# Streamed weights by single blocks in a ring of sixteen half-size slots

## The chip, the cores and the metric

The kernel runs on one core of a Trainium2 chip. The metric is the device time in microseconds from the first to the last instruction of that core. Five engines work beside each other: TensorE (PE, matmuls, with its weight loads listed as PEld), VectorE (DVE), ScalarE (ACT), GpSimd (POOL) and SyncE (SP), which here only issues transfers. Sixteen DMA engines carry the transfers between the chip's memory (HBM) and the on-chip buffer.

## The reference, cut to what matters

Two layers, each used twice in turn, A, B, A, B, with a residual around each. A is attention over segments of 32 tokens: each segment sees 8 memory tokens that come out of the segment before it, so the 64 segments of a layer are worked one after the other, and each needs all of the layer's weights (Wq, Wk, Wv and Wo, 31.5 MB together). B is a mixer with two small matmuls and a shift of tokens, followed by an MLP.

```python
# A: S = 2048 tokens, Dm = 640, H = 32 heads of Dh = 192, M = 8, seg_len = 32
for s in range(n_seg):
    xs = x[:, s * seg_len:(s + 1) * seg_len, :].copy()
    h = jnp.concatenate([mem, xs], axis=1)
    q = jnp.einsum('btd,dhe->bhte', h, Wq)
    k = jnp.einsum('btd,dhe->bhte', h, Wk)
    v = jnp.einsum('btd,dhe->bhte', h, Wv)
    scores = jnp.einsum('bhqe,bhke->bhqk', q, k) * scale
    scores = jnp.where(mask[None, None], scores, -1000000000.0)
    p = _softmax(scores, axis=-1)
    o = jnp.einsum('bhqk,bhke->bhqe', p, v)
    o = jnp.einsum('bhte,hed->btd', o, Wo)
    mem = o[:, :M, :].copy()
    outs.append(o[:, M:, :])
# B (D = 640, F = 1536)
h = _gelu(_layernorm(x, axis=-1) @ w1)
# ... hs = (h, each quarter of its columns shifted along the tokens) @ w2 ...
x1 = x + hs
h2 = _gelu(_layernorm(x1, axis=-1) @ w3) @ w4
# the whole: x + A(ln(x)), then x + B(ln(x)), then both once more
```

## The kernel before

Both uses of A run in one pass as two lanes: step t works segment t of the first use and segment t - 5 of the second, side by side in one matmul of 80 columns (2 x (32 + 8)), so a weight block that is loaded serves both. There are 64 + 5 = 69 steps. A step goes through eight groups of four heads. A weight block is 128 rows by 768 columns (k, q, v: five blocks a group) or 128 x 640 (o: six blocks a group, and all blocks of the mixer). The on-chip buffer doesn't hold all weights: of each group the first blocks stay (`CUT`), and the others are streamed from HBM at each step through a ring of slots.

```python
LAG = 5
HG = 4
RING = 8
RING_A = 7
RING_B = 3
CUT = {"k": [3] * 8, "q": [3] * 8, "v": [3] * 8, "o": [2] + [4] * 7}
# ...
DMA_RATE = 345.0e3
DMA_LAT = 2.2
DMA_SKEW = 1.6
FLIGHT = 5
```

`RING` is the number of slots of the ring; attention may hold 7 of them at once and the mixer 3. A slot has room for two blocks.

```python
    def ring(cls):
        b = Slotted(cls, None)
        b.make = lambda: wring.tile([P, 2 * GW], bf16, name="wst", tag=f"r{b.slot}")
        return b

    def block(t, kind, g, c, due):
        n = Dm if kind == "o" else GW
        cut = CUT[kind][g]
        if c < cut:
            # ... resident: one load of the first `cut` blocks, once ...
            return b, lambda: tl[:, c, :]
        a = cut + (c - cut) // 2 * 2
        if (t, kind, g, a) not in streamed:
            b = ring("ra")

            def fn(op):
                return nc.sync.dma_start(out=T(b)[:, 0:2 * n].rearrange("p (c n) -> p c n", c=2), in_=w_src(kind, g, a, a + 2))
            add("SP", 0.45, due, fn, w=(b,), dma=P * 2 * n * 2, queue="wa")
            streamed[t, kind, g, a] = b
        b = streamed[t, kind, g, a]
        return b, lambda: T(b)[:, (c - a) * n:(c - a + 1) * n]
```

`load_b` does the same for the mixer's blocks (w1, w2, w3, w4), also by twos. A block is used by a run of matmuls, of which each loads 128 x 128 of it:

```python
            for kc in range(KC):
                due = due0 + kc * 0.05
                wb, wv = block(t, "v", g, kc, due)

                def fv(op, wv=wv, kc=kc):
                    w, o = wv(), T(pv)
                    for c in range(GC):
                        nc.tensor.matmul(out=o[:, c, 0:N], lhsT=w[:, c * P:(c + 1) * P], rhs=h[:, kc, c0:c0 + N],
                                         start=pv.begin(), stop=True, skip_group_check=True)
```

The kernel doesn't write its instructions in program order. It records all operations with an estimated duration and a due time, lays them out on the engines once in Python (`Plan.place`), and then emits them in that fixed order. The plan, and at the end the program too, lets a weight transfer start only when the one `FLIGHT` places before it has landed:

```python
            if o.dma and o.e == "SP" and len(landed) >= FLIGHT:
                s = max(s, landed[-FLIGHT])
# ...
    for o in placed:
        ins = o.fn(o)
        if o.dma and o.e == "SP":
            if len(flight) >= FLIGHT:
                tc.add_manual_dep(ins.ins, flight[-FLIGHT].ins.name,
                                  mybir.DependencyInfo(mybir.DependencyClass.Sync, mybir.DependencyReason.DATA),
                                  reason="transfers in flight")
            flight.append(ins)
```

The semaphore waits that carry the order between engines and slots are set when the program is built.

Of the kernel before, what the change touches and what calls it, by code (L numbers as in the profile page):

```python
# [12 lines left out]
bf16 = mybir.dt.bfloat16  # L13
# [6 lines left out]

LAG = 5
HG = 4
RING = 8
RING_A = 7
RING_B = 3
CUT = {"k": [3] * 8, "q": [3] * 8, "v": [3] * 8, "o": [2] + [4] * 7}
YA = 3
STEP = 48.0
# [11 lines left out]
LOOK = 0.03  # L40
DMA_RATE = 345.0e3
DMA_LAT = 2.2
DMA_SKEW = 1.6
FLIGHT = 5


class Buf:
# [34 lines left out]
class Plan:  # L82
# [11 lines left out]
    def add(self, e, d, due, fn, r=(), w=(), a=(), dma=0, queue=None, after=()):  # L94
        op = Op()
        op.e, op.d, op.due, op.fn, op.dma = e, d, due, fn, dma
        op.succ, op.ready, op.n = [], 0.0, 0
        op.i = len(self.ops)
        preds = set(after)
        slots = []  # L100
        for b in r:
            preds.update(b.writers)
        for b in w:
            preds.update(b.writers)
            preds.update(b.readers)
        for b in a:
            preds.update(b.base)
            preds.update(b.readers)
        for b in r:
            b.readers.append(op)  # L110
        for b in w:
            b.base = [op]
            b.writers = [op]
            b.readers = []
        for b in a:
            b.writers.append(op)
        for b in {id(b): b for b in (*r, *w, *a)}.values():
            if isinstance(b, Slotted):
                b.left += 1
                slots.append(b)  # L120
        op.slots = slots
        preds.discard(op)
        for p in preds:
            p.succ.append(op)
            op.n += 1
        self.ops.append(op)
        if queue is not None:
            self.queues.setdefault(queue, []).append(op)
        return op

    def place(self):
# [28 lines left out]
        def est(o, t):  # L160
            s = max(t, o.ready)
            if o.dma and o.e == "SP" and len(landed) >= FLIGHT:
                s = max(s, landed[-FLIGHT])
            need = {}
# [11 lines left out]
        while left:  # L176
# [33 lines left out]
            if o.dma:  # L210
                srv = max(s + DMA_LAT, srv) + o.dma / DMA_RATE
                done = srv + DMA_SKEW
                if e == "SP":
# [33 lines left out]
def kernel(  # L247
# [16 lines left out]
    nc = tc.nc  # L264
    P = 128
    _, S, Dm = A_x.shape
# [5 lines left out]
    KC = Dm // P  # L272
    FC = F // P
    assert (Dm, F, Dh, H, SEG, M) == (640, 1536, 192, 32, 32, 8) and S % (2 * SEG) == 0 and NSEG > 8
    NG = H // HG
    GW = HG * Dh
# [6 lines left out]
    QD = Dm // 4  # L283
# [12 lines left out]
    w4_v = B_w4.rearrange("(c p) n -> p c n", p=P)  # L296
# [3 lines left out]
    wring = ctx.enter_context(tc.tile_pool(name="wring", bufs=1))  # L300
# [4 lines left out]
    wbd = dram.tile([KC + FC + 1, P, Dm], bf16, name="wbd")  # L305
# [74 lines left out]
    def B(*key):  # L380
        if key not in bufs:
            bufs[key] = Buf()
        return bufs[key]

    plan = Plan({**PSUM_BANKS, "r": RING}, {**PSUM_USES, "ra": ("r", RING_A), "rb": ("r", RING_B)})
    add = plan.add
# [9 lines left out]
    def T(b):  # L396
        if b.obj is None:
            b.obj = b.make()
        return b.obj
# [12 lines left out]
    def w_src(kind, g, a, e):  # L412
        if kind == "o":
            return Wo_v[:, g, a:e, :]
        return W_v[kind][:, a:e, GW * g:GW * (g + 1)]

    resident = {}
    streamed = {}

    def ring(cls):  # L420
        b = Slotted(cls, None)
        b.make = lambda: wring.tile([P, 2 * GW], bf16, name="wst", tag=f"r{b.slot}")
        return b

    def block(t, kind, g, c, due):
# [4 lines that stand above are left out]
            if (kind, g) not in resident:  # L430
                tl = wres.tile([P, cut, n], bf16, name=f"w{kind}{g}")
                b = Buf()

                def fn(op):
                    return nc.sync.dma_start(out=tl[:], in_=w_src(kind, g, 0, cut))
                add("SP", 0.45, due, fn, w=(b,), dma=P * cut * n * 2, queue="wa")
                resident[kind, g] = b, tl
            b, tl = resident[kind, g]
            return b, lambda: tl[:, c, :]
        a = cut + (c - cut) // 2 * 2  # L440
        if (t, kind, g, a) not in streamed:
            b = ring("ra")

            def fn(op):
                return nc.sync.dma_start(out=T(b)[:, 0:2 * n].rearrange("p (c n) -> p c n", c=2), in_=w_src(kind, g, a, a + 2))
            add("SP", 0.45, due, fn, w=(b,), dma=P * 2 * n * 2, queue="wa")
            streamed[t, kind, g, a] = b
        b = streamed[t, kind, g, a]
        return b, lambda: T(b)[:, (c - a) * n:(c - a + 1) * n]

    mixer = {}

    def load_b(c, nm, n, due):

        a = n - n % 2
        e = min(a + 2, KC if nm in ("w1", "w2") else FC)
        if (c, nm, a) not in mixer:
            b = ring("rb")
            k = {"w1": a, "w3": KC + a, "w2": KC + FC - 4 + a}.get(nm)
            if nm == "w4":  # L460
                src, rd = w4_v[:, a:e, :], []
            elif nm == "w2" and a < 4:
                src, rd = B_w2.rearrange("(g r) d -> r g d", r=QD)[0:P, a:e, :], []
            else:
                src = wbd[k:k + e - a].rearrange("b p n -> p b n")
                rd = [B("wbd", k + i) for i in range(e - a)]

            def fn(op):
                return nc.sync.dma_start(out=T(b)[:, 0:(e - a) * Dm].rearrange("p (c n) -> p c n", n=Dm), in_=src)
            add("SP", 0.45, due, fn, r=rd, w=(b,), dma=P * (e - a) * Dm * 2, queue="wb")  # L470
            mixer[c, nm, a] = b
        b = mixer[c, nm, a]
        return b, lambda: T(b)[:, (n - a) * Dm:(n - a + 1) * Dm]

    def order_mixer_weights():

# [35 lines left out]
    def attention_step(t):  # L512
# [11 lines left out]
        def proj_kq(g, s0):  # L524
            G = t * NG + g
            for kind, off in (("k", 0.0), ("q", 0.3 * sl)):
                pq = ps("P", [P, GC, NS], f32, "ps" + kind)
                now = []
                for kc in range(KC):
                    due = s0 + off + kc * 0.05  # L530
                    wb, wv = block(t, kind, g, kc, due)

                    def fn(op, pq=pq, wv=wv, kc=kc):
                        w, o = wv(), T(pq)
                        for c in range(GC):
                            nc.tensor.matmul(out=o[:, c, 0:N], lhsT=w[:, c * P:(c + 1) * P], rhs=h[:, kc, c0:c0 + N],  # L536
                                             start=pq.begin(), stop=True, skip_group_check=True)
                    now.append(add("PE", mm_us(N, k=GC), due, fn, r=(wb, *HX(t, kc)), a=(pq,), after=last[0]))
# [25 lines left out]
        def proj_v(g, due0):  # L564
# [5 lines left out]
# [9 lines that stand above are left out]
                now.append(add("PE", mm_us(N, k=GC), due, fv, r=(wb, *HX(t, kc)), a=(pv,), after=last[0]))  # L579
# [17 lines left out]
        def attend(g):  # L597
# [66 lines left out]
            held = g >= NG - OT_BUFS + 1  # L664
            at = base + STEP - HOLD + 0.5 * g if held else s0 + 1.9 * sl
            ws = [block(t, "o", g, c, at + 0.03 * c) for c in range(GC)]
            due = base + STEP - 1 + 0.02 * g if held else s0 + 2.0 * sl

# [178 lines left out]
    def chunk(c):  # L847
# [110 lines left out]
        for n in range(5):  # L958
            due = D(W2[0] + W2[1] * n)
            wb, wv = load_b(c, "w2", n, due)  # L960

            def fw(op, n=n, wv=wv):
                w = wv()
                off = W2OFF[n] if n < 4 else 0
                lhsT = hTB[:, n, off:off + TOK, :].rearrange("p w l -> p (w l)")
                for k in range(2):
                    nc.tensor.matmul(out=T(hs[k])[:], lhsT=lhsT, rhs=w[:, HC * k:HC * (k + 1)],  # L967
                                     start=hs[k].begin(), stop=True, skip_group_check=True)
            add("PE", mm_us(HC, k=2), due, fw, r=(wb, B("hTB", 0), B("hTB", 1)), a=tuple(hs))
# [130 lines left out]
# [6 lines that stand above are left out]
# [37 lines left out]
```

## Time and profile before

| | |
|---|---|
| time, median of three runs | 3589.97 us (3584.36 to 3591.39) |
| span of the profiled run | 3584.0 us |
| TensorE's granted clock, mean | 0.99 |
| moved by DMA | 1097 MB, 306 GB/s on average |
| shares of the chain that ended last | PE 86%, DMA 8%, issue 4% |
| streamed transfers | 2,277 pairs of attention blocks, 630 transfers of mixer blocks, 32 resident loads and 2 others |
| landing of a streamed attention pair, median | 5.0 to 5.2 us after its issue |

The page gives for each engine its busy time and share of the span; lists of waits give, for each group of instructions, what ended its idle time, with the sum in us, how often, and the longest. "issue" in place of a releaser means that nothing was found for which the engine waited. The DMA table counts packets: the rows of a transfer are packets of 1,536 or 1,280 bytes, and q1 is the queue that SyncE fills, q0 that of GpSimd, q8 and q14 carry instructions. In a timeline a row is a start, a duration, and the instructions merged in it. The transfer time to landing runs from the issue on SyncE to the last completion.

### The profile page before, as it was taken

The numbers are of one execution on the slowest core, as the hardware profiler recorded it, in microseconds if no ns is written. First come the engines' busy times: TensorE is split into PE (matmuls) and PEld (weight loads), VectorE is DVE, ScalarE is ACT, GpSimd is POOL, SyncE is SP. The second block draws the span as 40 slices with busy tenths as digits, with TensorE's granted clock in tenths as the row PEclk, the third lists the DMA queues.
The fourth block names the chain that finished last, engine by engine and source line by source line (L and its number), as shares of the span: only waits on it lengthen the run. The fifth ranks groups of instructions, "written<-read, shape, count | busy, mean of one in ns | idle before, by whom it ended". The sixth has DMA issues, their size and how long they took to land.

```text
span 3584.0 us, 188496 instructions
## 1 busy us (share of the span) xinstructions
PE 3387.8 (95%) x84703; PEld 3256.1 (91%) x84703; DVE 2375.3 (66%) x7085; ACT 1709.2 (48%) x3584; POOL 306.2 (9%) x522
## 2 busy tenths in 40 slices
PE   5889999999999999999999999999999999999996
PEld 4778999999999999999999999999999999999875
DVE  2456767767667666776666777776667667776555
ACT  2344545545455544455445554554545445544432
POOL 2000000000000000000000000000000000000000
PEclk9999999999999999999999999999999999999998
DMA  9999999999999999999999999999999999999996
GB/s 341 314 308 306 309 298 309 306 302 315 307 310 323 310 299 304 303 301 312 303 305 310 303 299 303 313 312 300 310 318 309 302 304 306 308 309 310 321 310 212
DMA packets 804793, 1097.18 MB, mean 306 GB/s; under 512 B 51982, under 2 KB 800540, under 8 KB 803984
## 3 DMA queue, kind: packets, MB, share of 16 engines
q1 hardware_dynamic: 795472, 1069.06, 91.2%
q0 software_dynamic: 8512, 16.08, 1.4%
q8 instruction: 662, 10.85, 1.2%
q14 instruction: 147, 1.20, 0.1%
HBM read 1079.68 MB, written 8.19 MB: 304 GB/s over the span
## 4 chain that ended last, share of the span: by engine, by line
PE 86%; DMA 8%; issue 4%; DVE 0%; ACT 0%; POOL 0%; SPq 0%; POOLq 0%; DVEq 0%; ACTq 0%
PE psy L675 16%; PE psk L536 15%; PE psv L577 15%; PE psq L536 15%; PE psvt L589 5%; PE pso L656 4%; PE pss L608 4%; PE psh L999 3%; DMA wst<-in_B_w_dram 3%; PE y L1017 3%; PE pst L641 2%; DMA wst<-in_A_Wk_dram 2%; PE hs L967 1%; DMA wst<-in_A_Wv_dram 1%; PE psh L945 1%
## 5 line engine op out<-in xcount | busy, mean ns | idle before, releaser
L536 PEld LDWEIGHTS <-wst 128*128 128x128 bf16 x13248 | 561.5, 100 | 36.0 <-issue 19.3
L662 DVE CAST oT<-pso 128x480 bf16<-128x480 f32 (+1 forms) x552 | 341.7, 619 | 379.7 <-PE pso L656 377.3
L593 ACT COPY V<-psvt 80x768 bf16<-80x768 bf16 (+1 forms) x552 | 438.4, 794 | 309.0 <-PE psvt L589 302.2
L675 PE MATMUL psy<-oT,wo 128*128 128x80 bf16 (+1 forms) x10350 | 491.6, 199 | 15.3 <-issue 8.6
L577 PE MATMUL psv<-hT,wv 128*128 128x80 bf16 (+1 forms) x9936 | 480.5, 199 | 12.3 <-issue 10.7
L544 ACT CAST qT<-psq 128x480 bf16<-128x480 f32 (+1 forms) x552 | 292.1, 529 | 400.5 <-PE psq L536 398.9
L536 PE MATMUL psq<-hT,wq 128*128 128x80 bf16 (+1 forms) x9936 | 454.2, 199 | 19.6 <-issue 10.0
L583 ACT CAST vTs<-psv 128x480 bf16<-128x480 f32 (+1 forms) x552 | 291.2, 528 | 362.7 <-PE psv L577 359.5
L536 PE MATMUL psk<-hT,wk 128*128 128x80 bf16 (+1 forms) x9936 | 452.8, 199 | 11.7 <-issue 9.3
L619 DVE CUSTOM_DVE_ANT_1 pss<-pss,mask 80x320 f32<-80x320 f32 (+1 forms) x512 | 246.0, 481 | 294.3 <-PE pss L608 287.8
L577 PEld LDWEIGHTS <-wv 128*128 128x128 bf16 x9936 | 408.4, 99 | 30.0 <-issue 11.0
L675 PEld LDWEIGHTS <-wo 128*128 128x128 bf16 x10350 | 413.3, 99 | 23.4 <-issue 15.3
L536 PEld LDWEIGHTS <-wq 128*128 128x128 bf16 x9936 | 395.2, 100 | 31.2 <-issue 13.3
L536 PEld LDWEIGHTS <-wk 128*128 128x128 bf16 x9936 | 397.9, 100 | 25.4 <-issue 14.3
L536 PE MATMUL psk<-hT,wst 128*128 128x80 bf16 (+1 forms) x6624 | 367.9, 199 | 12.1 <-issue 6.5
L577 PE MATMUL psv<-hT,wst 128*128 128x80 bf16 (+1 forms) x6624 | 353.2, 199 | 12.4 <-issue 8.2
L675 PE MATMUL psy<-oT,wst 128*128 128x80 bf16 (+1 forms) x6210 | 335.4, 199 | 11.2 <-issue 10.4
L536 PE MATMUL psq<-hT,wst 128*128 128x80 bf16 (+1 forms) x6624 | 331.6, 199 | 12.4 <-issue 9.4
L626 ACT ACTIVATE pss<-pss,sm 80x320 f32<-80x320 f32 (+1 forms) x552 | 262.0, 475 | 151.5 <-DVE sm L619 151.5
L631 DVE TENSOR_REDUCE sm<-pss 80x4 f32<-80x320 f32 (+1 forms) x552 | 252.3, 457 | 116.4 <-ACT pss L626 115.7
L552 DVE CAST kT<-psk 128x320 bf16<-128x320 f32 (+1 forms) x552 | 254.0, 460 | 112.7 <-PE psk L536 109.3
L646 ACT COPY PT<-pst 80x320 bf16<-80x320 bf16 (+1 forms) x552 | 221.9, 402 | 220.2 <-PE pst L641 218.1
(117 smaller groups left out, 5256.9 us busy)
## 6 DMA issues: line engine op xcount, KB each, us to landing
wst<-in_A_Wk_dram SPq DMA_DIRECT2D x552, 384.0 KB, 5.2
wst<-in_A_Wq_dram SPq DMA_DIRECT2D x552, 384.0 KB, 5.2
wst<-in_A_Wv_dram SPq DMA_DIRECT2D x552, 384.0 KB, 5.2
wst<-in_A_Wo_dram SPq DMA_DIRECT2D x621, 320.0 KB, 5.0
wst<-wbd SPq DMA_DIRECT2D x280, 320.0 KB, 5.1
wst<-in_B_w_dram SPq DMA_DIRECT2D x280, 320.0 KB, 5.7
wst<-wbd SPq DMA_DIRECT2D x70, 160.0 KB, 4.4
wk<-in_A_Wk_dram SPq DMA_DIRECT2D x8, 576.0 KB, 6.8
```

Source lines behind the costliest of these rows:

```text
L536: nc.tensor.matmul(out=o[:, c, 0:N], lhsT=w[:, c * P:(c + 1) * P], rhs=h[:, kc, c0:c0 + N], start=pq.begin(), stop=True, skip_group_check= ...
L544: nc.scalar.copy(out=q[:, :, 0:N], in_=T(pq)[:, :, 0:N])
L552: nc.vector.tensor_copy(out=k4[:, :, 0::3, 0:N], in_=p4[:, :, 0::2, 0:N])
L577: nc.tensor.matmul(out=o[:, c, 0:N], lhsT=w[:, c * P:(c + 1) * P], rhs=h[:, kc, c0:c0 + N], start=pv.begin(), stop=True, skip_group_check= ...
L583: nc.scalar.copy(out=vs[:, :, 0:N], in_=T(pv)[:, :, 0:N])
L593: nc.scalar.copy(out=V_[0:N, :, 0:Dh], in_=T(pt)[0:N].rearrange("n c f -> n (c f)").rearrange("n (i e) -> n i e", i=HG))
L619: nc.vector.tensor_tensor_reduce(out=o, in0=o, in1=maskt.unsqueeze(1).to_broadcast([N, HG, N]), scale=-scale, scalar=3.0e38, op0=ALU.add, ...
L626: nc.scalar.activation(out=o, in_=o, func=ACT.Exp, bias=sm_[0:N, 0:1], scale=-1.0)
L631: nc.vector.reduce_sum(out=sm_[0:N, 4:4 + HG], in_=o, axis=AX.X)
L646: nc.scalar.copy(out=Pt[0:N, :, 0:N], in_=T(pst)[0:N, :, 0:N])
L662: nc.vector.tensor_copy(out=o_[:, :, 0:N], in_=T(pso)[:, :, 0:N])
L675: nc.tensor.matmul(out=T(psy[j])[:, m - m0, c0:c0 + N], lhsT=w[:, m * P:(m + 1) * P], rhs=o_[:, c, 0:N], start=psy[j].begin(), stop=True, ...
```

## The change

Each streamed block becomes a transfer of its own, into a slot of half the size; the ring has sixteen of these, with the same bytes in all. A slot then comes free after one block is used and not after two, TensorE can start on a block without waiting for its neighbour, and the mixer's odd blocks (w1 and w2 have five) leave no half of a slot empty. The limit on transfers in flight is set to sixteen. The plan's estimates of an issue on SyncE and of the time to landing are adjusted. A switch for issuing the mixer's loads from GpSimd is added, and stays off (`B_SP = True`). What is computed, which blocks stay resident and the number of matmuls are unchanged.

```diff
--- before.py
+++ after.py
@@ -20,9 +20,12 @@
 
 LAG = 5
 HG = 4
-RING = 8
-RING_A = 7
-RING_B = 3
+RING = 16
+RING_A = 14
+RING_B = 6
+B_SP = True
+POOL_US = 0.9
+SP_US = 0.47
 CUT = {"k": [3] * 8, "q": [3] * 8, "v": [3] * 8, "o": [2] + [4] * 7}
 YA = 3
 STEP = 48.0
@@ -40,8 +43,8 @@
 LOOK = 0.03
 DMA_RATE = 345.0e3
 DMA_LAT = 2.2
-DMA_SKEW = 1.6
-FLIGHT = 5
+DMA_SKEW = 2.0
+FLIGHT = 16
 
 
 class Buf:
@@ -419,7 +422,7 @@
 
     def ring(cls):
         b = Slotted(cls, None)
-        b.make = lambda: wring.tile([P, 2 * GW], bf16, name="wst", tag=f"r{b.slot}")
+        b.make = lambda: wring.tile([P, GW], bf16, name="wst", tag=f"r{b.slot}")
         return b
 
     def block(t, kind, g, c, due):
@@ -433,44 +436,35 @@
 
                 def fn(op):
                     return nc.sync.dma_start(out=tl[:], in_=w_src(kind, g, 0, cut))
-                add("SP", 0.45, due, fn, w=(b,), dma=P * cut * n * 2, queue="wa")
+                add("SP", SP_US, due, fn, w=(b,), dma=P * cut * n * 2, queue="wa")
                 resident[kind, g] = b, tl
             b, tl = resident[kind, g]
             return b, lambda: tl[:, c, :]
-        a = cut + (c - cut) // 2 * 2
-        if (t, kind, g, a) not in streamed:
+        if (t, kind, g, c) not in streamed:
             b = ring("ra")
 
             def fn(op):
-                return nc.sync.dma_start(out=T(b)[:, 0:2 * n].rearrange("p (c n) -> p c n", c=2), in_=w_src(kind, g, a, a + 2))
-            add("SP", 0.45, due, fn, w=(b,), dma=P * 2 * n * 2, queue="wa")
-            streamed[t, kind, g, a] = b
-        b = streamed[t, kind, g, a]
-        return b, lambda: T(b)[:, (c - a) * n:(c - a + 1) * n]
-
-    mixer = {}
+                return nc.sync.dma_start(out=T(b)[:, 0:n], in_=w_src(kind, g, c, c + 1)[:, 0, :])
+            add("SP", SP_US, due, fn, w=(b,), dma=P * n * 2, queue="wa")
+            streamed[t, kind, g, c] = b
+        b = streamed[t, kind, g, c]
+        return b, lambda: T(b)[:, 0:n]
 
     def load_b(c, nm, n, due):
 
-        a = n - n % 2
-        e = min(a + 2, KC if nm in ("w1", "w2") else FC)
-        if (c, nm, a) not in mixer:
-            b = ring("rb")
-            k = {"w1": a, "w3": KC + a, "w2": KC + FC - 4 + a}.get(nm)
-            if nm == "w4":
-                src, rd = w4_v[:, a:e, :], []
-            elif nm == "w2" and a < 4:
-                src, rd = B_w2.rearrange("(g r) d -> r g d", r=QD)[0:P, a:e, :], []
-            else:
-                src = wbd[k:k + e - a].rearrange("b p n -> p b n")
-                rd = [B("wbd", k + i) for i in range(e - a)]
-
-            def fn(op):
-                return nc.sync.dma_start(out=T(b)[:, 0:(e - a) * Dm].rearrange("p (c n) -> p c n", n=Dm), in_=src)
-            add("SP", 0.45, due, fn, r=rd, w=(b,), dma=P * (e - a) * Dm * 2, queue="wb")
-            mixer[c, nm, a] = b
-        b = mixer[c, nm, a]
-        return b, lambda: T(b)[:, (n - a) * Dm:(n - a + 1) * Dm]
+        b = ring("rb")
+        k = {"w1": n, "w3": KC + n, "w2": KC + FC - 4 + n}.get(nm)
+        if nm == "w4":
+            src, rd = w4_v[:, n, :], []
+        elif nm == "w2" and n < 4:
+            src, rd = B_w2[QD * n:QD * n + P, :], []
+        else:
+            src, rd = wbd[k], [B("wbd", k)]
+
+        def fn(op):
+            return (nc.sync if B_SP else nc.gpsimd).dma_start(out=T(b)[:, 0:Dm], in_=src)
+        add("SP" if B_SP else "POOL", SP_US if B_SP else POOL_US, due, fn, r=rd, w=(b,), dma=P * Dm * 2, queue="wb")
+        return b, lambda: T(b)[:, 0:Dm]
 
     def order_mixer_weights():
```

## The prediction

> **What bounds the kernel now.** I read the page's busy table first, then the DMA table, then the busy time by stretch, then the list of what TensorE waited for, then the timeline of one such wait.
>
> ```profile
> PE 3387.8 (95%) x84703; PEld 3256.1 (91%) x84703; DVE 2375.3 (66%) x7085; ACT 1709.2 (48%) x3584; POOL 306.2 (9%) x522
> ...
> q1 hardware_dynamic: 795472, 1069.06, 91.2%
> q0 software_dynamic: 8512, 16.08, 1.4%
> q8 instruction: 662, 10.85, 1.2%
> ```
>
> TensorE is busy for 3388 of 3584 us. The change leaves its 84,703 weight loads and 84,703 matmuls as they are, so all that can be won is the 3584 - 3388 = 196 us in which it is idle. The DMA engines are occupied nearly as long, so the weight stream looks like the other candidate for the bound. The stretch of the steady steps and TensorE's waits in it say whether it is.
>
> ```profile
> core 0: us, PE busy (x) PEld busy (x) DVE busy (x) ACT busy (x) POOL busy (x), PEclk, DMA share, GB/s
> 300.00:3300.00 3000.00, 2917.22 (x72643) 2846.38 (x72641) 2097.03 (x6064) 1502.25 (x3073) 248.22 (x416) 1.00 0.94 307
> ```
>
> ```profile
> PE psy L675 <- issue: 15.5, 25, 1.4
> PE psq L536 <- issue: 13.1, 21, 2.6
> PE psv L577 <- issue: 13.1, 19, 2.2
> PE y L1017 <- DMA wst<-in_B_w_dram: 10.8, 13, 1.7
> PE psk L536 <- issue: 9.2, 18, 1.1
> ...
> PE psk L536 <- DMA wst<-in_A_Wk_dram: 2.2, 7, 0.5
> ...
> PE psv L577 <- DMA wst<-in_A_Wv_dram: 1.5, 2, 1.2
> ```
>
> The steady 3000 us hold 83 us of idle TensorE. Waits on weights are 10.8 + 2.2 + 1.5 = 14.5 us of it. Most of the rest is called "issue", which means that the profile shows nothing that was waited for. One such wait in the timeline:
>
> ```profile
> 1504.91 0.34 PE L577 MATMUL psv<-hT,wv 128*128 128x80 bf16 x5
> ...
> 1506.63 0.21 PE L577 MATMUL psv<-hT,wv 128*128 128x80 bf16 x1 [1.38 <-issue]
> ```
>
> The matmuls before and after the hole use the same resident tile and the same accumulator, so no data can be missing. I therefore counted TensorE's instructions from the start of the trace. Of 288 holes over 0.35 us between weight loads, 148 stand at one place modulo 256 instructions (193 or 194). And the DMA table's queue q8, "instruction", moved 662 packets; 10.85 MB / 662 is 16 KB, and 169,406 loads and matmuls / 662 is 256 of them per packet. So these holes are TensorE waiting for its next 16 KB of program. Adding them over all 658 boundaries that I could place gives 132 us: two thirds of the whole idle time (23 us before 300 us, 91 in the steady stretch, 18 after it; these are holes between weight loads and come out slightly longer than PE's own idle). **The weights are not the bound; the program's own loading is the largest removable term**, and it shares the DMA engines with the weights.
>
> [...] The trace of before says that it matters somewhat: from a boundary to the start of the next 16 KB packet it took 1.60 us on average with three weight transfers open at the boundary, 2.01 with four, 2.41 with five, and the stall that followed averaged 80, 107 and 281 ns. [...]
>
> **The change, part by part.** *Number of transfers.* Pairs of 384 or 320 KB become single blocks of 192 or 160 KB. In the built order SyncE issues 5,778 transfers where it had 2,941; bytes and row lengths stay. In the trace one issue holds SyncE for 0.423 us on average, and the shortest distance between two issues is 0.46 us, so about 0.09 lies around an issue: 5,778 x (0.423 + 0.09) = 2,970 us, 83% of the span, against 42% before. There is room, and SyncE is not on TensorE's path while the ring is ahead. Each transfer also ends in a 9 ns packet on each DMA engine: 2,837 x 9 ns = 26 us per engine, 0.7% of the span, beside other work.
>
> *Transfers in flight.* Read in the built order, "up to sixteen" is not what comes out. The transfers take eight completion semaphores in turn, and each waits for its predecessor on the same one:
>
> ```
> 2998 L447 DMACopy wst<-in_A_Wq_dram 128x768 [waits DMAHW7_49,PE_49]
> 2999 L447 DMACopy wst<-in_A_Wv_dram 128x768 [waits DMAHW0_49,PE_49]
> ```
>
> So the true limit is eight. Before, each waits for the one five before it. In bytes: before 5 x 366 KB = 1.83 MB at most (1.55 MB on average by issues and landings in the trace); after 8 x 183 KB = 1.46 MB at most, perhaps 1.3 on average. The depth of the weight queue falls by a fifth, though the change was meant to raise it. That is as in the "four transfers open" class of before, or a little below it: a stall of about 0.10 us per boundary in place of 132/658 = 0.20. Over the 613 boundaries after 300 us, where stalls are now 91 + 18 = 109 us (0.18 each), this leaves about 613 x 0.10 = 61 us: **-48 us**. Up to 300 us the large resident loads keep the queue as deep as before, so I take nothing there. Half-size transfers also break the queue up more finely, which could help further; I add nothing for it.
>
> *The ring.* Sixteen half slots hold the same bytes, but each comes free after one block. I measured the lead in the built order as the number of matmuls between the release of a slot and the first use of what is loaded into it: median 208 before, 225 after, lowest hundredth 111 and 132. At 0.0406 us a matmul (18 weight loads in 0.73 us in the timeline) the lowest hundredth goes from 4.5 to 5.4 us, and the median landing is
>
> ```profile
> wst<-in_A_Wk_dram SPq DMA_DIRECT2D x552, 384.0 KB, 5.2
> ```
>
> So the latest transfers come out better: **-5 us** of the 14.5 us, an estimate. Against it stands the smaller limit in flight: 1.46 MB at 307 GB/s must be issued, land and be followed up within 4.8 us, where 160 KB alone took 2.3 us at the start. That holds on average; for bad moments I put **+5 us**. The sum is 3585 - 48 - 5 + 5, about 3537; I say 3535.
>
> **Rivals.** (1) *The fetch delay does not follow the weight queue.* Then the stalls stay at 132 us. For it: [...] the wide scatter of the delay (10% to 90%: 1.1 to 3.2 us). The time would be 3580 to 3590. (2) *The smaller limit in flight or SyncE's 83% starves the ring.* For it: 20% of the issues already take more than 0.4 us, and SyncE works strictly in order. Against it: SyncE's waits for a slot that TensorE still holds are its largest before, so the ring is usually full. If the weight waits quadrupled, +45 us would eat the gain: about 3585; beyond that 3620 and more. (3) *Finer packets help fetches more than depth does*: the stalls nearly vanish after 300 us, 3585 - 100, about 3485.
>
> **Range and chances.** The centre takes the measured dependence on depth at face value. Rival 1 sets the upper end, 3590; rival 3 with a little left over sets the lower, 3490. Faster by over 2% means below 3518, which needs about 70 us of the 109: 0.30. Slower by over 2% needs rival 2 in full: 0.05. The rest, 0.65, is within 2%.
>
> **What would show it.** Right: PE's busy time within 10 us of 3388; "issue" waits in the steady stretch down from about 63 us to 30 to 40; stalls at the 256-instruction boundaries at about 60 us after 300 us; landings of 4.0 to 4.6 us; weight waits of TensorE below 25 us in the steady stretch. Wrong: weight waits of 50 us or more (then lead or issue rate was misjudged), or boundary stalls unchanged although fewer bytes are open (then the queue's depth was not their cause).

## The result and the profile after

The changed kernel takes 3692 us (median; 3680 to 3703), the kernel before 3588: a ratio of 1.029 (95% interval 1.025 to 1.033). It is slower by almost 3%, outside the predicted range of 3490 to 3590. In the profiled runs the span grew from 3584.0 to 3701.2 us.

The page's busy table and the weights' queue in the changed kernel; in the queue line stand packets, MB and the share of the 16 engines' span:

```profile
span 3701.2 us, 194162 instructions
...
PE 3424.2 (93%) x84703; PEld 3281.0 (89%) x84703; DVE 2376.2 (64%) x7085; ACT 1714.7 (46%) x3584; POOL 305.9 (8%) x522
...
q1 hardware_dynamic: 840864, 1069.24, 89.7%
```

The weights are the same 1069 MB and the DMA engines are a little less occupied than before, although TensorE now waits for weights. What TensorE waited for in the same steady 3000 us (us in total, times, longest):

```profile
PE y L1011 <- DMA wst<-in_B_w_dram: 52.2, 59, 2.8
PE psh L993 <- DMA wst<-wbd: 48.9, 30, 3.3
PE psq L530 <- ACT V L587: 20.4, 28, 0.7
PE psv L571 <- DMA wst<-in_A_Wv_dram: 16.2, 20, 1.5
PE psk L530 <- DMA wst<-in_A_Wk_dram: 8.4, 15, 1.6
PE psq L530 <- DMA wst<-in_A_Wq_dram: 6.0, 11, 1.7
PE psv L571 <- issue: 0.6, 1, 0.6
...
PE psk L530 <- issue: 0.3, 1, 0.3
```

The two lists, before and after, have changed places. "issue" fell from 63 us to about 1: the holes at the 256-instruction boundaries went from 132 us to 12 over the whole span, far more than predicted. Weights, 14.5 us before, now cost 52.2 + 48.9 + 16.2 + 8.4 + 6.0 = 132 us. Over the whole span the 117 us of growth are, by the waits and the busy time: waits on DMA, nearly all of them for weights, 45.8 to 199.9 (+154), "issue" 98.9 to 6.6 (-92), TensorE's busy time 3387.8 to 3424.2 (+36), the rest +19 (of which psq's wait for ScalarE's copy of V, 20 us in the steady stretch, is the only large new one).

The steady stretch and the transfers, each transfer with its size and its median time to landing:

```profile
300.00:3300.00 3000.00, 2843.40 (x70339) 2770.73 (x70338) 2032.39 (x5871) 1461.83 (x2980) 240.91 (x402) 0.99 0.93 298
```

```profile
wst<-in_A_Wk_dram SPq DMA_DIRECT2D x1104, 192.0 KB, 4.4
wst<-in_A_Wq_dram SPq DMA_DIRECT2D x1104, 192.0 KB, 4.5
wst<-in_A_Wv_dram SPq DMA_DIRECT2D x1104, 192.0 KB, 4.5
wst<-in_A_Wo_dram SPq DMA_DIRECT2D x1242, 160.0 KB, 4.3
```

A block half the size lands only 0.7 us sooner than a pair did (5.0 to 5.2 us). SyncE's own timeline shows how closely it now works; "x2" with 0.86 us is two issues back to back:

```profile
1518.76 0.86 SPq L447 DMA_DIRECT2D wst<-in_A_Wv_dram  x2
1519.71 0.38 SPq L465 DMA_DIRECT2D wst<-in_B_w_dram  x1
1520.18 0.86 SPq L447 DMA_DIRECT2D wst<-in_A_Wk_dram  x2
```

I split SyncE's time in the steady stretch by its instruction records. Before, it waited 26% of the time for a landing and 29% for TensorE to free a slot: the ring was mostly full. After, it waits 6% for a landing and 3% for a slot, and for the rest issues: one issue holds it for 0.472 us (0.423 before) plus about 0.093 around it, 0.565 us a block. With 183 KB a block that is 324 GB/s at most. The average need is 1069 MB in TensorE's 3388 busy us, 315 GB/s. So SyncE has little to spare: of the 307 GB/s of the kernel before in this stretch some 299 are the weights' (1069 of 1097 MB), and issuing them alone would take 299/324 = 92% of its time. With 9% of waits that can't be held, and the stretch comes to 298 GB/s in all.

In the trace of the changed kernel SyncE's 5,778 issues take eight completion semaphores in turn, without an exception, and at most eight transfers are open at once; before, it was five. So two causes were open. **Theory A, bytes in flight:** these eight transfers are 1.46 MB, too little to keep up the rate. **Theory B, issue rate:** SyncE, at 324 GB/s and with its issues in that fixed order, has no room to catch up. Further rivals were small transfers as such, and an order laid out for a stream that doesn't come.

### The profile page after: what moved, and what is told of

It reads as the page before. It is cut to its first block, busy times and chain, and to the rows that moved or that the text cites. A ratio compares the mean times of both kernels' runs of the same rounds, so it can differ in the third digit from the quotient of the medians.

```text
span 3701.2 us, 194162 instructions
## 1 busy us (share of the span) xinstructions
PE 3424.2 (93%) x84703; PEld 3281.0 (89%) x84703; DVE 2376.2 (64%) x7085; ACT 1714.7 (46%) x3584; POOL 305.9 (8%) x522
## 3 DMA queue, kind: packets, MB, share of 16 engines
q14 instruction: 192, 1.57, 0.1%
## 4 chain that ended last, share of the span: by engine, by line
PE 72%; DMA 25%; issue 2%; ACT 1%; POOL 0%; SPq 0%; DVE 0%; POOLq 0%; DVEq 0%
PE psy L669 14%; PE psk L530 13%; PE psq L530 12%; PE psv L571 12%; DMA wst<-in_B_w_dram 5%; DMA wst<-in_A_Wq_dram 5%; DMA wst<-wbd 5%; DMA wst<-in_A_Wv_dram 5%; PE psvt L583 4%; PE pss L602 4%; DMA wst<-in_A_Wk_dram 3%; PE pso L650 3%; PE psh L993 3%; PE y L1011 2%; PE pst L635 2%
## 5 line engine op out<-in xcount | busy, mean ns | idle before, releaser
L530 PEld LDWEIGHTS <-wst 128*128 128x128 bf16 x13248 | 551.0, 100 | 55.2 <-DMA wst<-in_A_Wk_dram 28.5
L669 PE MATMUL psy<-oT,wo 128*128 128x80 bf16 (+1 forms) x10350 | 502.2, 200 | 8.0 <-DMA wo<-in_A_Wo_dram 5.0
L571 PE MATMUL psv<-hT,wv 128*128 128x80 bf16 (+1 forms) x9936 | 471.4, 199 | 4.4 <-DMA wv<-in_A_Wv_dram 3.1
L669 PEld LDWEIGHTS <-wo 128*128 128x128 bf16 x10350 | 422.5, 100 | 11.7 <-DMA wo<-in_A_Wo_dram 6.1
L530 PE MATMUL psk<-hT,wst 128*128 128x80 bf16 (+1 forms) x6624 | 354.8, 199 | 22.8 <-DMA wst<-in_A_Wk_dram 21.2
L669 PE MATMUL psy<-oT,wst 128*128 128x80 bf16 (+1 forms) x6210 | 346.5, 201 | 6.8 <-DMA wst<-in_A_Wo_dram 5.3
L530 PE MATMUL psq<-hT,wst 128*128 128x80 bf16 (+1 forms) x6624 | 334.0, 199 | 16.2 <-DMA wst<-in_A_Wq_dram 13.9
```

Source lines behind the costliest of these rows:

```text
L669: nc.tensor.matmul(out=T(psy[j])[:, m - m0, c0:c0 + N], lhsT=w[:, m * P:(m + 1) * P], rhs=o_[:, c, 0:N], start=psy[j].begin(), stop=True, ...
```

## The experiments

Each diff is against the kernel before (names b_) or the changed one (names a_). "Stalls" are the holes at the 256-instruction boundaries; "weights" is the sum of TensorE's waits on DMA over the whole span of the profiled run (of which some 7 us, the same in every run, are a wait for another input). Each ratio is to runs of the kernel before that were made together with it, whose medians lie between 3579 and 3588 us; so differences of a few us between rows mean nothing.

| run | us | ratio to before (95%) | stalls | weights |
|---|---|---|---|---|
| before | 3588 | | 132 | 46 |
| changed | 3692 | 1.029 (1.025 to 1.033) | 12 | 200 |
| b_flight4 | 3691 | 1.031 (1.028 to 1.034) | 14 | 147 |
| b_drain9 | 3555 | 0.993 (0.990 to 0.995) | 57 | 82 |
| a_pool | 3579 | 0.999 (0.998 to 1.001) | 46 | 79 |
| a_plan8 | 3662 | 1.023 (1.020 to 1.027) | 10 | 172 |
| a_pool_cap8 | 3757 | 1.048 (1.043 to 1.053) | 7 | 190 |
| b_drain11 | 3719 | 1.039 (1.035 to 1.043) | 11 | 241 |
| b_flight6 | 3618 | 1.011 (1.006 to 1.016) | 152 | 51 |
| b_flight45 | 3689 | 1.029 (1.023 to 1.034) | 34 | 141 |
| b_drain10 | 3619 | 1.009 (1.006 to 1.012) | 22 | 140 |
| b_real4 | 3711 | 1.035 (1.029 to 1.040) | 18 | 225 |
| a_pool_cap10 | 3590 | 0.999 (0.997 to 1.002) | 30 | 97 |
| b_drain6 | 3537 | 0.986 (0.982 to 0.991) | 75 | 53 |

### b_flight4: the same bytes in flight, in pairs

```diff
-FLIGHT = 5
+FLIGHT = 4
```

> The kernel before with one number changed: four pairs in flight in place of five, 1.46 MB, the same bytes as eight single blocks; SyncE still issues 2,941 transfers. If the smaller number of bytes in flight is what starves the ring after the change, TensorE waits for weights for 100 us or more and the time is 3650 to 3700 us. If it is SyncE's issue rate, nothing starves; the stalls at the 256-instruction boundaries fall from 132 us to 60 to 80 and the time is 3520 to 3560.

3691 us, the time of the changed kernel, with half its transfers. SyncE has time to spare: it waits 56% of the steady stretch for a landing and under 1% for a slot. TensorE's waits in the steady stretch:

```profile
PE psy L675 <- DVE oT L662: 35.9, 60, 0.7
PE psk L536 <- DMA wst<-in_A_Wk_dram: 30.0, 52, 2.3
PE psq L536 <- DMA wst<-in_A_Wq_dram: 18.1, 32, 1.5
PE psv L577 <- DMA wst<-in_A_Wv_dram: 14.3, 27, 1.3
...
PE pso L656 <- issue: 1.0, 1, 1.0
```

For pairs, then, a limit of 1.46 MB is enough for a loss of this size, without any shortage of issue rate. One line doesn't fit: the waits on oT, of which the kernel before has 0.8 us in all. The plan has laid out its order for four as well, and b_real4 separates that.

### b_drain9: a slow issue alone

```diff
+IDLE = 9
         ins = o.fn(o)        # at the end, where the instructions are emitted; ahead of it:
+        if o.dma and o.e == "SP":
+            for _ in range(IDLE):
+                tc.nc.sync.drain()
```

> The kernel before with nine empty instructions (drains) ahead of each of SyncE's transfers, so that an issue costs it about twice as long, some 1.1 us, and SyncE is occupied for some 90% of the span as after the change. Transfers, slots, order and bytes in flight are those of before. Issue rate as the cause: TensorE waits for weights for 100 us or more and the time is 3650 to 3720 us. Bytes in flight, small transfers or the order of the plan as the cause: 3580 to 3600, as before.

Neither: 3555 us, *faster* than before. An issue now takes 1.09 us a pair (336 GB/s at most), SyncE is occupied 90% of the span, and the waits for weights are 82 us where they were 46. Being busy is thus no great harm by itself. The gain comes from the stalls, 132 to 57 us: the pairs no longer go out in bursts, and 1.49 MB are open on average in the steady stretch where it was 1.57.

### a_pool: single blocks, the mixer's issued by GpSimd

```diff
-B_SP = True
+B_SP = False
```

> The changed kernel with its own switch set: the mixer's 1,190 single blocks are issued by GpSimd, which is idle 92% of the time, and SyncE issues 4,588 transfers in place of 5,778 (occupied about 70%). The same single blocks and ring. Issue rate as the cause: the weight waits mostly go, the boundary stalls stay below 40 us, 3490 to 3560 us. Small transfers as such (overhead in the DMA engines): no change, 3670 to 3700. Bytes in flight as the cause: in part better, 3600 to 3680, as GpSimd's transfers come on top of the eight.

3579 us, between the two bands. The same single blocks through two queues lose nothing, so small transfers as such are not the cause. But GpSimd's transfers take eight completion semaphores of their own (in the traces of before and of the changed kernel each of these has 31 or 32 of GpSimd's 250 transfers): 8.2 transfers of both queues and 1.47 MB are open on average against 7.4 and 1.32 in the changed kernel, and for a tenth of the time it is 1.87 MB or more. It relieves both suspects, and a_pool_cap8 was made to part them.

### a_plan8: an order that knows the limits

```diff
-SP_US = 0.47
+SP_US = 0.565
-FLIGHT = 16
+FLIGHT = 8
```

> The changed kernel with the plan told the truth: eight transfers in flight in place of sixteen, and 0.565 us for an issue in place of 0.47. Number of transfers and the true limit in flight stay. If the fixed order was laid out for a stream that the chip cannot deliver and a fitting order heals it: 3560 to 3620 us. If SyncE's rate itself is the limit, an order can hide little of it: 3660 to 3700.

3662 us. The order is worth 20 to 30 of the 104 us (by the ratios and by the times); most of the loss is not the order's.

### a_pool_cap8 and a_pool_cap10: relief for SyncE, with and without bytes

```diff
+CAP = 8                                     # 10 in a_pool_cap10; both with B_SP = False
+    ring_b = {o.i for o in plan.queues["wb"]}
-        if o.dma and o.e == "SP":
-            if len(flight) >= FLIGHT:
-                tc.add_manual_dep(ins.ins, flight[-FLIGHT].ins.name,
+        if o.dma and (o.e == "SP" or o.i in ring_b):
+            if len(flight) >= CAP:
+                tc.add_manual_dep(ins.ins, flight[-CAP].ins.name,
```

> The kernel of a_pool (mixer blocks issued by GpSimd, SyncE 4,588 transfers), with one wait more: of the ring's transfers of both queues together no more than eight are open. So SyncE is relieved as in a_pool, and the bytes in flight are limited to 1.46 MB as in the changed kernel. If SyncE's issue rate is what made the changed kernel slow, the relief stays: 3560 to 3610 us. If it is the bytes in flight, the time goes back: 3660 to 3700 us.

3757 us, above both bands: with 20% fewer issues on SyncE but eight transfers open in all, nothing of a_pool's relief is left. SyncE waits again, 21% of the steady stretch, for landings. Another 30 us of TensorE's idle time there is a wait of the mixer's normalisation (psn for vb) that is 1.8 us in a_pool; that GpSimd now waits for landings too is a likely reason.

> As a_pool_cap8 with ten of the ring's transfers open, 1.83 MB at most, the limit of the kernel before. If bytes in flight decide, most of the way from 3757 back to a_pool's 3579: 3580 to 3650 us, boundary stalls 15 to 45 us. If the cross waits between the two queues are what made a_pool_cap8 slow, it stays above 3700.

3590 us. Two transfers more bring back 168 us. That is not all due to the weights: a_pool_cap8 is 65 us slower than the changed kernel under the same limit, so part of its loss belongs to the waits between the queues, which a limit of ten loosens too (the waits of psn for vb fall from 30 us to 3.4). What the pair shows for single blocks is that relief of SyncE under a limit of eight gains nothing, and that with ten open the loss is gone.

### b_real4 and b_flight45: four pairs without the plan, and the middle

```diff
-            if len(flight) >= FLIGHT:                     # b_real4, in the program only
-                tc.add_manual_dep(ins.ins, flight[-FLIGHT].ins.name,
+            if len(flight) >= 4:
+                tc.add_manual_dep(ins.ins, flight[-4].ins.name,
```

```diff
-                s = max(s, landed[-FLIGHT])               # b_flight45, in the plan and the program
+                s = max(s, landed[-FLIGHT + len(landed) % 2])
```

> The kernel before in its own fixed order (laid out for five pairs in flight), but the program lets only four be open. b_flight4 had changed the order too. If four pairs are too few for the chip whatever the order: 3680 to 3760 us, weight waits above 100 us. If b_flight4's time came from the order made for four: 3550 to 3600.

3711 us in the old order, and TensorE's longest waits in the steady stretch are now for weights alone:

```profile
PE y L1017 <- DMA wst<-in_B_w_dram: 54.3, 44, 2.6
PE psk L536 <- DMA wst<-in_A_Wk_dram: 43.9, 58, 2.1
```

Four pairs are too few here whatever the order. Transfers, slots, order and issue cost are those of the kernel before; this is the cleanest run on the limit. The 20 us by which b_flight4 is faster lie within the intervals of the two ratios.

> The kernel before with the limit alternating between four and five pairs from transfer to transfer, 1.65 MB on average. Four pairs starve TensorE of weights (3691), five make it wait for instructions. If both costs vary smoothly with depth, the middle is better than either: boundary stalls of 30 to 60 us, weight waits of 40 to 80, 3530 to 3580 us. If four is already the edge of starving: 3600 to 3650.

3689 us, missed: the middle as tried is no better than four. It is no clean middle, though. With this rule a transfer and the next one wait for the same landing, so the pairs go out by twos: the distance between two issues is 0.46 and 1.78 us in turn (medians), where it was 1.08 before. And the order was laid out anew, with 32 us of waits on oT as in b_flight4. How sharp the edge between four and five is stays open.

### b_flight6: more depth

```diff
-FLIGHT = 5
+FLIGHT = 6
```

> The kernel before with six pairs in flight, 2.2 MB. If stalls at instruction boundaries follow the depth of the weight queue, they rise from 132 us to 200 us or more and the time is 3620 to 3700 us, although the weights come sooner. If they don't follow it: 3570 to 3590.

3618 us, just under the band, and the stalls rose only to 152 us. The direction holds, the size was overestimated: with the ring's eight slots the average open rose from 1.57 to 1.59 MB only, though what is reached or exceeded for a tenth of the time went from 1.90 to 2.13.

### b_drain11, b_drain10, b_drain6: the issue rate as a dose

```diff
-IDLE = 9
+IDLE = 11      # 10 and 6 in the others
```

> As b_drain9, with eleven empty instructions: an issue costs SyncE about 1.22 us a pair, 300 GB/s at most, where b_drain9 allowed 336 and the changed kernel 324. If an issue rate close under the need of 315 GB/s is enough to cost what the change cost, the time is 3680 to 3850 us, with SyncE hardly ever waiting. If the issue rate isn't a bound, it stays near b_drain9's 3555.

3719 us. At 1.19 us a pair (308 GB/s, under the need of 315) the issue rate binds: TensorE's waits on DMA are 241 us where they were 46.

> As b_drain9 with ten empty instructions. From b_drain9 and b_drain11 each costs 0.05 us, so a pair costs SyncE 1.14 us, 321 GB/s: the pace of the changed kernel (0.565 us a block, 324 GB/s), but with five pairs allowed in flight, 1.83 MB, in place of eight single blocks, 1.46 MB. If the changed kernel's pace alone explains its time: 3670 to 3700 us. If the limit in flight is what hurts, and the pace only below need: 3560 to 3610.

3619 us, between the bands and 9 us off the one for the limit. This is the changed kernel's average pace, 321 GB/s against 324, with 1.83 MB allowed in flight: 73 us better than the changed kernel. Its weight waits of 140 us, partly offset by the stalls, which fell from 132 to 22, show that the pace does cost something; against the kernel before it is 33 us, a third of the 104 us of the change. On average 1.42 MB are open in its steady stretch, no more than in b_flight4 (1.44) and b_real4 (1.42), which take 3691 and 3711 us: the average is thus not what decides over the weights; that the limit does, when SyncE has to catch up, fits.

> As b_drain9 with six empty instructions: 0.94 us a pair, 389 GB/s at most, above what the DMA engines deliver. It is the search for the better side: if spacing out the issues is what takes the boundary stalls away (132 to 57 us with nine), six keep part of that (70 to 100 us) with fewer weight waits than nine: 3540 to 3575 us. If only a pace near the need does it, it is as before, 3575 to 3590.

3537 us, a ratio of 0.986 (0.982 to 0.991): **better than both kernels.** The 389 GB/s of the expectation stand against 343 GB/s in the first 100 us of before, where the DMA share was 1.00. The page of this run, and its steady stretch (in the order in which the columns stood before):

```profile
PE 3385.8 (96%) x84703; PEld 3259.7 (92%) x84703; DVE 2375.8 (67%) x7085; ACT 1709.6 (48%) x3584; POOL 306.9 (9%) x522
```

```profile
300.00:3300.00 3000.00, 2946.34 (x73572) 2875.54 (x73569) 2119.66 (x6149) 1518.43 (x3116) 249.50 (x419) 1.00 0.95 311
```

```profile
PE y L1018 <- DMA wst<-in_B_w_dram: 9.5, 21, 1.6
PE psk L537 <- issue: 8.1, 13, 1.6
PE psy L676 <- issue: 7.8, 17, 1.0
PE psq L537 <- issue: 5.5, 11, 0.9
PE psv L578 <- DMA wst<-in_A_Wv_dram: 4.1, 5, 2.6
```

The steady stretch has 54 us of idle TensorE where it had 83; "issue" halved, from 63 to 30 us, and weights rose only from 14.5 to 20. The drains compute nothing, take about 0.05 us each (1.09 us a pair with nine, 1.19 with eleven) and are a crude way to space out issues. That they help is what the run shows; whether by the even spacing or by the somewhat smaller number of bytes open (1.55 MB on average against 1.57) is not separated.

Over all runs the stalls follow the bytes open on average in the steady stretch closely: 1.59 MB 152 us, 1.57 MB 132, 1.55 MB (b_drain6) 75, 1.49 MB (b_drain9) 57, 1.47 MB (a_pool) 46, 1.42 MB (b_drain10) 22, 1.32 MB (changed) 12, 1.29 MB (a_pool_cap8) 7. b_flight45 (1.52 MB, 34 us) and b_flight4 (1.44 MB, 14 us) lie below that line. No run changes the average alone.

## Why the prediction was wrong, point by point

**The stalls at instruction boundaries: right in kind, too small.** That TensorE's unnamed waits are its own program arriving late can be read from the trace of before packet by packet. One packet of program is fetched after each boundary (662 of 16 KB in all), and TensorE goes on 1.4 us (median) after the end of the packet that was fetched at the boundary before; of the 134 stalls over 0.3 us, 132 come out of this sum. That the stalls shrink when fewer weight bytes are open held too: 132 us with five pairs, 14 to 18 with four, 152 with six. I put the gain at 48 us; it was 120, and it came in the first 300 us as well (23 to 2), where I had expected none. I had taken the stall of moments with four pairs open in the kernel before (0.107 us). But such a moment mostly stands beside moments with five. Under a standing limit of four, the median delay from a boundary to the next program packet fell from 2.15 us to 1.47, and the stall to 14 us / 653 boundaries = 0.02 us. A class picked out of one run is not what a run held in that class does. What makes the delay change with the load like this is not shown.

**Transfers in flight: the limit was read rightly, its cost was not.** The step that failed is "Against it stands the smaller limit in flight ... That holds on average; for bad moments I put **+5 us**". The term came out at +154 us of weight waits, whatever SyncE's pace adds to them included. I had compared 4.8 us, the time in which 1.46 MB must turn over at 307 GB/s, with the 2.3 us of a transfer alone. The time that counts is that of a transfer among others, and the kernel before already had it, for the mixer's odd blocks:

```profile
wst<-wbd SPq DMA_DIRECT2D x70, 160.0 KB, 4.4
```

I had even named 4.0 to 4.6 us as the landings to expect. Put into the sum they leave 0.4 us for the semaphore, the issue and a late landing, and +5 us would not have stood. For pairs the limit alone is enough: b_real4 loses 125 us by it. Four pairs landing in 4.9 us give 1.46 MB / 4.9 us = 298 GB/s (b_flight4 moved 300 in the steady stretch, all queues together), under the need of 315; five in 5.1 us give 359. For eight blocks the same sum gives 1.46 / 4.4 = 332 GB/s, 5% above the need. So the limit leaves the changed kernel next to no room rather than none.

**SyncE "is not on TensorE's path while the ring is ahead": true, and the ring was no longer ahead.** This is the second step that failed, "There is room". The occupation, predicted 83%, was 88% of a longer span, because an issue took 0.472 us and not 0.423. The old kernel's ring was full since SyncE could run ahead at 366 KB per 0.52 us. b_drain10 gives the worth of such a pace alone: about 33 us net. In the changed kernel SyncE stands 6% of the steady stretch waiting for a landing, against 56% in b_flight4: there the limit is the plain bound, here issuing and waiting together fill SyncE's time.

**The longer lead in the ring (-5 us) and finer packets (rival 3)** are not seen. A few us of lead can't be told under a loss of this size. The stalls nearly vanished, as rival 3 said, but with the same 1.46 MB allowed, pairs (b_flight4, 14 us) and single blocks (12 us) stall alike, so it is not the fineness.

**PE's busy time, "within 10 us of 3388":** it was 36 us more. In the clock records TensorE ran at half speed for 140 us in all against 72 before, in pieces of 3.4 us and multiples, eleven of them in the steady stretch where there was one at its edge. Half of the additional 68 us is 34. That would do here; in b_flight4, however, the busy time rose by 47 us with only 31 us more at half speed, so what else lengthens it stays open.

**The rivals.** Rival 2 named both causes, a starved ring by the limit or by SyncE, and gave them 5%. What spoke against it, SyncE's waits for slots, was a property of the old kernel with its 1.83 MB and 42% occupation; the change took away both.

What stays open is how the two causes share the changed kernel's loss. Each alone was measured in other surroundings: the limit with pairs, and the pace with evenly spaced issues, while those of the changed kernel take 0.32 us at least and 9% of them over 1 us. No run has all 5,778 issues on SyncE and more than eight transfers open.

## What to carry to other kernels

A limit on open transfers is a limit on bytes, and with a fixed number of them it halves with the size of a transfer (here eight blocks are 1.46 MB, where five pairs were 1.83): look at what the built program waits for, not at the constant in the source. Work out the margin from the landing time under load (bytes allowed / landing time against the rate needed), not from a transfer alone; landing time itself moves with the depth (the median was 4.4 us for a block, 4.9 and 5.2 for a pair among four, b_flight4, and five, before), so leave room, and count the issuing engine's time as well. Where TensorE has holes that nothing explains, count its instructions: where they stand 256 apart, try a more evenly spaced weight stream. Here that was worth 1.4%, while a greater and a smaller depth both lost.

## What the runs showed of the hardware that was not expected

- A fifth fewer bytes allowed in flight cost 125 us with nothing else changed: 1.83 MB 3586 us, 1.46 MB 3711 us (b_real4).
- A transfer's sixteen completions come spread over 1.8 us at the median in the changed kernel (first at 2.6 us, last at 4.4 after the issue of a 192 or 160 KB block) and over 1.9 us before (3.2 and 5.2 for a pair), so the spread hardly shrank with the size. Of a 192 KB block twelve completions are in after 3.6 us and the last after 4.5; in neither trace does a transfer start on a semaphore before the last completion of the one before it on the same, so a block counts as open for 0.9 us after three quarters of its completions. That is a likely reason why half-size transfers don't land in half the time; no run isolates it.
- Slowing SyncE by six drains a transfer made the kernel 1.4% faster (b_drain6: 3537 us, a ratio of 0.986).
